# Converting float64 weights to float32 inside a Trainium2 kernel: a scaled absolute value in place of a raise and a mask

## The chip, the cores and the metric

The kernel runs on one core of a Trainium2 chip. A core has a matrix engine (PE), a vector engine (DVE), a scalar engine for activations and copies (ACT), a general one (POOL), and a queue of DMA issues on SyncE (SP). Each takes its instructions strictly in the order in which they stand in its program; semaphores hold an instruction until what it needs is there. The metric is the device time of one execution in microseconds.

## The reference, cut to what matters

Attention with packed queries p, then a mixer along the sequence (U, V) and a two-layer perceptron (w1, w2), for 8 batches, 8 heads, 576 rows, 64 columns a head.

```python
def _attn_ref(q, k, v, p):
    def sm_attn(qq, kk, vv):
        s = scale * np.matmul(qq, kk.transpose(0, 1, 3, 2))
        s = s - np.max(s, axis=-1, keepdims=True)
        a = np.exp(s)
        a = a / (np.sum(a, axis=-1, keepdims=True) + 1e-09)
        return np.matmul(a, vv)
    p_packed = sm_attn(p, k, v)
    out = sm_attn(q, p_packed, p_packed)

def _moe_ref(x, U, V, w_ch1, w_ch2):
    h = x.transpose(0, 2, 1) @ U @ V
    u = x + h.transpose(0, 2, 1)
    return u + np.maximum(u @ w_ch1, 0.0) @ w_ch2
```

q, k, v and p are float32. U, V, w1 (512 x 2048) and w2 (2048 x 512) are float64 and reach the kernel as pairs of 32-bit words; the kernel turns them into float32 itself, and this conversion is what the change is about.

## The kernel before, in words

**Stage 1 (to 98.3 us in the profile)** goes over 16 units, two for each batch. A unit loads its share of k (tile kx, three buffers, issue at L218) and of v (vt, three buffers, L425 and L427). It turns k by PE transposes (L229, L239) that ACT (L236, L240) and DVE (L234) copy out to kT. It forms scores with the packed queries (PE L249 into s_ps, one buffer), takes their maximum (DVE L460), the exponential (ACT L462), transposes it back (PE L255 and L257; ACT L471 and L474 copy it to eT), multiplies by v (PE L490), scales (ACT L492) and puts the heads in place (POOL L493, PE L500, ACT L501). Once a batch the packed queries are prepared: p is loaded (pn, one buffer, L415), doubled on POOL (L433, tile pd), transposed on PE (L435) and copied with the attention's scale by ACT (L436, L439) to pT, which both units of the batch use in L249.

Spread over the units stand 16 conversions of blocks of w1 (128 x 512 each), two small ones of U and V, and the conversion of w2's first block with its split into a high and a low part (ACT L165, and for this block POOL L166). With unit 13 the first fold is written: w1 times the packed result of batch 0 (PE L384), cut into a high part (ACT L390) and a low part (DVE L391). In stage 1 the order on each engine isn't that of the code: a scheduler places the instructions by their dependencies and its own costs, for the whole stage at once, so that a change in one operation's form can move others on every engine.

**Stage 2 (98.3 us to the end)** stands in the order in which it is written. It holds, for each batch, 16 pairs of a product with the folded w1 (PE L87 to L89 into h_ps, taken out by ACT L634 and L636 and DVE L637) and one with w2 (L87 to L89 into o). Between them stand the conversions of w2's other 15 blocks (up to about 180 us; the low half of their split is on DVE, L166), the steps of the next batch's attention, and the fold for what comes next. PE starts stage 2 with the first L87 into h_ps.

**A conversion** takes the high and the low word of each float64. It is called three ways: `convert_w1` (its Abs having been done ahead by `test_w1`, L150), `convert_w2` and `prepare_uv`. Before, it has one ACT instruction and four on DVE: Abs of the high word read as a float (L78 or L150), the raise to the least number that float32 shall hold (L79, `max`), the shift by 3 with a mask that keeps it clear of the sign (L80), the sign and top exponent bit from the high word (L81), and the top 3 bits of the low word (L82).

Of the kernel before, what the change touches and what calls it, by code (L numbers as in the profile page):

```python
# [9 lines left out]
F32 = mybir.dt.float32  # L10
F32R = mybir.dt.float32r
I32 = mybir.dt.int32
AF = mybir.ActivationFunctionType
ALU = mybir.AluOpType
# [6 lines left out]
def packed_attention_mixer_kernel(  # L21
# [27 lines left out]
    nc = tc.nc  # L49
# [13 lines left out]
    scale = 1.0 / float(D) ** 0.5  # L63
# [1 line left out]
    HALF = (slice(0, 5 * I), slice(5 * I, S))  # L65
    LAST = slice(4 * I, 5 * I)

    LEAST = 1.125 * 2.0 ** -15

    U, V, w1, w2 = (a.bitcast(I32) for a in (U, V, w1, w2))  # L70

    def float32_of(x, t, raw, out=None, tested=False):


        low, high = raw[:, :, 0], raw[:, :, 1]
        out = x if out is None else out.bitcast(I32)
        if not tested:
            nc.scalar.activation(t, high.bitcast(F32), AF.Abs)  # L78
        nc.vector.tensor_single_scalar(t, t, LEAST, op=ALU.max)  # L79
        nc.vector.tensor_scalar(x, t.bitcast(I32), 3, 0x3FFFFFF8, op0=ALU.logical_shift_left, op1=ALU.bitwise_and)  # L80
        nc.vector.scalar_tensor_tensor(x, high, -0x40000000, x, op0=ALU.bitwise_and, op1=ALU.bitwise_or)  # L81
        nc.vector.scalar_tensor_tensor(out, low, 29, x, op0=ALU.logical_shift_right, op1=ALU.bitwise_or)  # L82
        return out.bitcast(F32)

# [47 lines left out]
    def conv_tile(dtype):  # L132
        return pipe.tile([P, DM], dtype, name="os", bufs=4)
# [5 lines left out]
    bits = {}  # L139
# [6 lines left out]
    tests = {}  # L146

    def test_w1(n):
        tests[n] = conv_tile(F32)
        nc.scalar.activation(tests[n], bits["w1", n][:, :, 1].bitcast(F32), AF.Abs)  # L150

    def convert_w1(n):
        x, c = chunks[n]
        float32_of(conv_tile(I32), tests.pop(n), bits.pop(("w1", n)), w1t[x][:, QW * c:QW * c + QW], tested=True)
# [5 lines left out]
    def convert_w2(kt):  # L160
        return kt, float32_of(conv_tile(I32), conv_tile(F32), bits.pop(("w2", kt)))
# [26 lines left out]
    def prepare_uv(ub, vbits):  # L188
        ux = float32_of(conv_tile(I32)[:, :5 * R], conv_tile(F32)[:, :5 * R], ub.rearrange("p (x t) -> p x t", t=2))
        for (n, ks) in ((P, slice(0, 4)), (64, slice(4, 5))):  # L190
            nk = ks.stop - ks.start
            src = ux.rearrange("p (k r) -> p k r", k=5)[:n, ks].unsqueeze(2).to_broadcast([n, nk, 4, R])
            nc.vector.tensor_copy(ua4[:n, ks], src)
            nc.vector.tensor_tensor(ua4[:n, ks, 1], src[:, :, 0], ua4[:n, ks, 0].bitcast(F32), op=ALU.subtract)
        n = I // 2
        w = S // 4
        vq = float32_of(conv_tile(I32)[:, :w], conv_tile(F32)[:, :w], vbits.rearrange("p (x t) -> p x t", t=2))
        spread = x_tile()[:, :4 * P].rearrange("p (q a r) -> p q a r", q=4, a=4)
        nc.gpsimd.tensor_copy(spread, ident.rearrange("p (r q) -> p q r", q=4).unsqueeze(2).to_broadcast([P, 4, 4, R]))
        spread = spread.rearrange("p q a r -> p q (a r)")  # L200
        for hf in range(2):
            v_ps = bank()
            for y in range(2):
                nc.tensor.matmul(v_ps[:, w * y:w * y + w], lhsT=spread[:, 2 * hf + y], rhs=vq, start=True, stop=True)
            vx = v_ps[:, :2 * w].rearrange("p (i c) -> p i c", c=NT)
            blocks = vx[:, :, :8].rearrange("p i (a k r) -> p r k i a", a=2, k=2)
            ns = slice(n * hf, n * hf + n)
            pairs = [(vs[:, LAST][:, ns], vx[:, :, 8])]
            for r in range(2):
                dst = vs[:, HALF[r].start:HALF[r].start + 4 * I].rearrange("p (k i a) -> p k i a", k=2, a=2)[:, :, ns]  # L210
                pairs.append((dst, blocks[:, r]))
            for dst, src in pairs:
                nc.scalar.copy(dst, src)
                nc.vector.tensor_tensor(dst[96:], src[96:], dst[96:].bitcast(F32), op=ALU.subtract)
# [304 lines left out]
    a_turn(0)  # L519
    first = attention(0, res)  # L520
    test_w1(0)

    def some_w1(n):
        convert_w1(n)
        if n + 1 < 16:
            test_w1(n + 1)
        if n + 4 < 16:
            load_w1(n + 4)
# [182 lines left out]
    for b in range(B):  # L711
# [3 lines left out]
        for kt in range(NK):  # L715
# [17 lines left out]
            if kt % 4 == 2 and (b, kt) != (B - 1, NK - 2):  # L733
                n = b * NPC + kt // 4 + 1
# [58 lines left out]
```

## Time and profile before

| | us |
|---|---|
| time, median of 3 runs (829.01 to 829.96) | 829.05 |
| span of the profiled execution | 827.6 |
| stage 1, first load to first L87 | 98.3 |
| PE busy in the span | 799.1 |

One execution is profiled. Its span is the time from the first to the last recorded instruction; the time of a run includes a little around it. Timeline rows read: start in us, duration in us, engine, line, operation, output tile, input tiles, shape, count, and in brackets the engine's idle time before it with what ended it. In rows of groups, the count is followed by busy time in us and the mean duration in ns.

### The profile page before, as it was taken

To read this page: it belongs to the slowest core of one execution; us is meant where nothing else is said; L and a number is where in the kernel's file an instruction comes from. 1 tells how busy PE (TensorE), PEld (TensorE's weight loads), DVE (VectorE), ACT (ScalarE), POOL (GpSimd) and SP (SyncE) were. 2 spreads that over 40 slices of the span, in tenths; PEclk is the share of its full clock that TensorE was granted. 3 is DMA by queue.
4 is the path that set the end of the run, shared out by engine and by line. 5 is a ranking of instruction groups with operands and counts; after the bars stand their busy time and mean duration, and the time that the engine had idled before them with its cause. 6 is when DMAs were issued, how large, how long until landed. Compare 5 with 4: busy or idle time off the path is not lost.

```text
span 827.6 us, 15457 instructions
## 1 busy us (share of the span) xinstructions
PE 799.1 (97%) x6224; PEld 644.8 (78%) x6224; DVE 364.6 (44%) x815; ACT 319.8 (39%) x974; POOL 81.3 (10%) x115
## 2 busy tenths in 40 slices
PE   7788889999999999999999999999999999999997
PEld 5456567778888888888888888888888888887886
DVE  3789677783343333433334234333434234332232
ACT  5788764444223332333233232343234232332231
POOL 0222201100111001010101001010101011100000
PEclk8999999999999999999999999999999999999999
DMA  9999863216002220023002120122002200030001
GB/s 295 347 363 349 272 163 98 77 51 188 2 1 68 80 55 2 1 96 93 1 1 96 51 55 1 60 84 46 2 30 85 75 14 1 15 111 1 2 0 64
DMA packets 60310, 70.23 MB, mean 85 GB/s; under 512 B 22864, under 2 KB 41296, under 8 KB 60240
## 3 DMA queue, kind: packets, MB, share of 16 engines
q1 hardware_dynamic: 59920, 68.73, 26.6%
q8 instruction: 49, 0.80, 0.4%
q10 hardware_dynamic: 320, 0.52, 0.2%
q14 instruction: 21, 0.17, 0.1%
HBM read 53.64 MB, written 15.60 MB: 84 GB/s over the span
## 4 chain that ended last, share of the span: by engine, by line
PE 87%; DVE 5%; ACT 2%; DMA 1%; issue 1%; POOL 0%; ACTq 0%
PE o L87 16%; PE o L89 16%; PE o L88 16%; PE h_ps L87 9%; PE h_ps L89 8%; PE h_ps L88 8%; PE t_ps L384 4%; PE o L654 2%; PE t_ps L229 2%; PE t_ps L249 1%; DVE os L81 1%; PE t_ps L327 1%; PE t_ps L255 1%; DMA kx<-in_k_dram 1%; PE t_ps L344 1%
## 5 line engine op out<-in xcount | busy, mean ns | idle before, releaser
L87 PE MATMUL o<-w2h,hh 128*128 128x512 f32 x512 | 207.0, 404 | 0.0
L89 PE MATMUL o<-w2h,hl 128*128 128x512 f32 x512 | 202.9, 396 | 0.0
L88 PE MATMUL o<-w2l,hh 128*128 128x512 f32 x512 | 202.3, 395 | 0.0
L637 DVE SCALAR_TENSOR_TENSOR hl<-h_ps,hh 128x256 fp32r<-128x256 f32 x256 | 105.3, 423 | 203.3 <-ACT hj L636 189.3
L634 ACT ACTIVATE hh<-h_ps 128x256 fp32r<-128x256 f32 x256 | 98.8, 387 | 183.2 <-PE h_ps L89 182.5
L87 PE MATMUL h_ps<-ah,wth 128*128 128x320 f32 (+1 forms) x512 | 157.6, 308 | 0.8 <-DVE hl L637 0.8
L88 PE MATMUL h_ps<-al,wth 128*128 128x320 f32 (+1 forms) x512 | 151.5, 296 | 0.0
L89 PE MATMUL h_ps<-ah,wtl 128*128 128x320 f32 (+1 forms) x512 | 151.3, 296 | 0.0
L87 PEld LDWEIGHTS h_ps<-ah,wth 128*128 128x128 f32 x512 | 96.6, 189 | 26.2 <-issue 20.2
L89 PEld LDWEIGHTS o<-w2h,hl 128*128 128x128 f32 x512 | 96.6, 189 | 22.6
L87 PEld LDWEIGHTS o<-w2h,hh 128*128 128x128 f32 x512 | 97.3, 190 | 21.1 <-issue 4.6
L88 PEld LDWEIGHTS o<-w2l,hh 128*128 128x128 f32 x512 | 97.2, 190 | 16.8
L88 PEld LDWEIGHTS h_ps<-al,wth 128*128 128x128 f32 x512 | 96.8, 189 | 2.0
L89 PEld LDWEIGHTS h_ps<-ah,wtl 128*128 128x128 f32 x512 | 97.0, 189 | 0.0
L391 DVE TENSOR_TENSOR wtl<-t_ps,wth 128x256 fp32r<-128x256 f32 x128 | 48.5, 420 | 101.1 <-ACT wth L390 97.8
L390 ACT CAST wth<-t_ps 128x256 fp32r<-128x256 f32 x128 | 43.3, 374 | 109.3 <-PE t_ps L384 102.6
L347 POOL TENSOR_TENSOR al<-aT,ah 128x320 fp32r<-128x320 f32 (+1 forms) x32 | 25.7, 809 | 210.8 <-ACT ah L346 210.8
L290 POOL TENSOR_TENSOR e<-e,m 128x576 f32<-128x576 f32 x16 | 18.6, 1165 | 260.9 <-DVE m L289 259.1
L236 ACT COPY xT<-t_ps 128x256 f32<-128x256 f32 x64 | 21.3, 392 | 39.5 <-PE t_ps L229 38.8
L384 PE MATMUL t_ps<-w1t,ppT 64*32 64x512 f32 x512 | 34.9, 601 | 0.0
L346 ACT CAST ah<-aT 128x320 fp32r<-128x320 f32 (+1 forms) x32 | 13.8, 435 | 43.7 <-DVE aT L345 43.7
L636 ACT ACTIVATE hj<-h_ps 128x64 f32<-128x64 f32 x128 | 28.2, 220 | 0.0
(122 smaller groups left out, 838.3 us busy)
## 6 DMA issues: line engine op xcount, KB each, us to landing
bits<-in_moe_w_ch_dram SPq DMA_DIRECT2D x32, 512.0 KB, 6.2
kx<-in_k_dram SPq DMA_DIRECT2D x16, 576.0 KB, 7.2
x<-in_q_dram SPq DMA_DIRECT2D x16, 576.0 KB, 5.1
vt<-in_v_dram SPq DMA_DIRECT2D x32, 256.0 KB, 6.8
out_dram<-bits SPq DMA_DIRECT2D x32, 256.0 KB, 2.4
aD<-aT SPq DMA_DIRECT2D x16, 288.0 KB, 2.1
aP<-aD SPq DMA_DIRECT2D x32, 128.0 KB, 3.1
ppP<-ppD SPq DMA_DIRECT2D x32, 64.0 KB, 3.0
```

Of the source, the lines that this page charges most:

```text
L87: nc.tensor.matmul(ps, lhsT=lh, rhs=rh, start=start, stop=False)
L88: nc.tensor.matmul(ps, lhsT=lh, rhs=rl, start=False, stop=False)
L89: nc.tensor.matmul(ps, lhsT=ll, rhs=rh, start=False, stop=stop)
L236: nc.scalar.copy(dst, src[:, a])
L290: nc.gpsimd.tensor_tensor(e, e, m.unsqueeze(2).to_broadcast([P, S // 32, 32]), op=ALU.subtract)
L347: nc.gpsimd.tensor_tensor(al[:, g, ns], aT[:, ns], ah[:, g, ns].bitcast(F32), op=ALU.subtract)
L384: nc.tensor.matmul(f_ps[g][xs], lhsT=ppT[b][zs, g, xs], rhs=w1t[h // 2][zs, QW * c:QW * c + QW], start=True, stop=True)
L390: nc.scalar.copy(hi[:, g], f_ps[g][:, cs])
L391: nc.vector.tensor_tensor(lo[:, g], f_ps[g][:, cs], hi[:, g].bitcast(F32), op=ALU.subtract)
L634: nc.scalar.activation(hh[:, ms], src, AF.Relu)
L636: nc.scalar.activation(hj[:, jslot(self.b, kt), self.js], h_ps[:, LAST], AF.Relu)
L637: nc.vector.scalar_tensor_tensor(hl[:, ms], src, 0.0, hh[:, ms].bitcast(F32), op0=ALU.max, op1=ALU.subtract)
```

## The change

The Abs on ACT gets a scale of 2^-112, which its own instruction applies. With it the high word's exponent comes out in the place where float32 wants it, so the raise (L79) is gone, the shift (L80) has no mask any more and writes from the scaled value, and L81 takes the sign bit alone instead of the sign and the top exponent bit. Line numbers behind L79 stand as before; Abs inside `float32_of` is L79 after the change.

```diff
-    LEAST = 1.125 * 2.0 ** -15
+    REBIAS = 2.0 ** -112
+    SIGN = -0x80000000
...
         if not tested:
-            nc.scalar.activation(t, high.bitcast(F32), AF.Abs)
-        nc.vector.tensor_single_scalar(t, t, LEAST, op=ALU.max)
-        nc.vector.tensor_scalar(x, t.bitcast(I32), 3, 0x3FFFFFF8, op0=ALU.logical_shift_left, op1=ALU.bitwise_and)
-        nc.vector.scalar_tensor_tensor(x, high, -0x40000000, x, op0=ALU.bitwise_and, op1=ALU.bitwise_or)
+            nc.scalar.activation(t, high.bitcast(F32), AF.Abs, scale=REBIAS)
+        nc.vector.tensor_single_scalar(x, t.bitcast(I32), 3, op=ALU.logical_shift_left)
+        nc.vector.scalar_tensor_tensor(x, high, SIGN, x, op0=ALU.bitwise_and, op1=ALU.bitwise_or)
         nc.vector.scalar_tensor_tensor(out, low, 29, x, op0=ALU.logical_shift_right, op1=ALU.bitwise_or)
...
     def test_w1(n):
         tests[n] = conv_tile(F32)
-        nc.scalar.activation(tests[n], bits["w1", n][:, :, 1].bitcast(F32), AF.Abs)
+        nc.scalar.activation(tests[n], bits["w1", n][:, :, 1].bitcast(F32), AF.Abs, scale=REBIAS)
```

In stage 2 the rows on every engine are the same but for the L79 rows, which are gone. In stage 1 the scheduler places the work anew. The end of stage 1 shows it best, where the conversion of w2's first block (bits_1676 before, bits_1659 after) meets the packed queries of units 14 and 15 (pd and pT). Numbers in the names count tiles, and so differ between the two programs for the same thing: pd_1498 and pd_1484, pT_1497 and pT_1483, e1_1527 and e1_1513 (unit 13's exponential) go together.

On ACT, at the end of stage 1, this stood before:

```order
L78 ACTIVATE os_1687<-bits_1676 128x512
L236 COPY kT_1611<-k_ps_1612 128x2x128 x2
L462 ACTIVATE e1_1527,sm_1423<-s_ps_1483,sm_1423 128x576
L236 COPY kT_1611<-k_ps_1619 128x2x128
L436 ACTIVATE pT_1497<-t_ps_1496 128x128
L439 ACTIVATE pT_1497<-t_ps_1496 128x2x32 x2
L501 COPY ppTa_1560<-t_ps_1561 128x128
L477 ACTIVATE sm_1423<-sm_1423,eps_71 128x2
L492 ACTIVATE two_1557<-m_ps_1536,sm_1200 128x128
L240 COPY kT_1611<-k_ps_1626 64x4x64
L471 COPY eT_1586<-m_ps_1587 128x512
L165 CAST w2h0_102<-os_1686 128x512
```

And this stands there now:

```order
L236 COPY kT_1596<-k_ps_1597 128x2x128 x2
L462 ACTIVATE e1_1513,sm_1411<-s_ps_1469,sm_1411 128x576
L236 COPY kT_1596<-k_ps_1604 128x2x128
L477 ACTIVATE sm_1411<-sm_1411,eps_71 128x2
L492 ACTIVATE two_1542<-m_ps_1521,sm_1190 128x128
L240 COPY kT_1596<-k_ps_1611 64x4x64
L471 COPY eT_1571<-m_ps_1572 128x512
L79 ACTIVATE os_1670<-bits_1659 128x512
L474 COPY eT_1571<-m_ps_1578 64x128
L165 CAST w2h0_102<-os_1669 128x512
L436 ACTIVATE pT_1483<-t_ps_1482 128x128
L439 ACTIVATE pT_1483<-t_ps_1482 128x2x32 x2
```

The Abs of w2's first block has moved behind the copy of unit 13's transposed exponential (L471), and the scaled copies to pT (L436, L439) have moved behind the block's cast (L165). Behind them on ACT now follow unit 14's exponential and then the four casts of the fold, the two of one bank next to each other; before, the fold's casts stood on both sides of that exponential.

On POOL, at the same place, this stood before:

```order
L433 COPY pd_1498<-pn_1419 128x256
L347 TENSOR_TENSOR al_1261<-aT1_1132,ah_1260 128x320
L347 TENSOR_TENSOR al_1261<-aT0_926,ah_1260 128x256
L347 TENSOR_TENSOR al_1261<-aT1_1132,ah_1260 128x256
L493 COPY ppall_73<-two_1557 128x64
L166 TENSOR_TENSOR w2l0_103<-os_1686,w2h0_102 128x512
L493 COPY ppall_73<-two_1669 128x64
```

And this stands there now:

```order
L347 TENSOR_TENSOR al_1250<-aT1_1122,ah_1249 128x320
L347 TENSOR_TENSOR al_1250<-aT0_918,ah_1249 128x256
L347 TENSOR_TENSOR al_1250<-aT1_1122,ah_1249 128x256
L493 COPY ppall_73<-two_1542 128x64
L166 TENSOR_TENSOR w2l0_103<-os_1669,w2h0_102 128x512
L433 COPY pd_1484<-pn_1407 128x256
L493 COPY ppall_73<-two_1652 128x64
```

The doubling of p (L433) has moved from ahead of the mixer's subtractions (L347) to behind the low half of w2's first block (L166).

On PE, before, the transposes of pd (L435) stood well ahead of unit 14's scores (s_ps_1598):

```order
L435 MATMUL t_ps_1496<-ident_66,pd_1498 128x128 x2
L500 MATMUL t_ps_1561<-ident_66,two_1466 128x128
L490 MATMUL m_ps_1536<-vt_1173,eT_1375 32x64 x20
L239 MATMUL k_ps_1626<-ident_66,kx_1524 64x128 x2
L255 MATMUL m_ps_1587<-ident_66,e1_1527 128x128 x4
L249 MATMUL s_ps_1598<-kT_1505,pT_1497 32x320
```

Now they stand right ahead of them (s_ps_1583):

```order
L490 MATMUL m_ps_1521<-vt_1163,eT_1363 32x64 x20
L239 MATMUL k_ps_1611<-ident_66,kx_1510 64x128 x2
L255 MATMUL m_ps_1572<-ident_66,e1_1513 128x128 x4
L257 MATMUL m_ps_1578<-ident_66,e1_1513 64x128
L490 MATMUL m_ps_1631<-vt_1275,eT_1459 32x64 x20
L435 MATMUL t_ps_1482<-ident_66,pd_1484 128x128 x2
L500 MATMUL t_ps_1546<-ident_66,two_1452 128x128
L249 MATMUL s_ps_1583<-kT_1491,pT_1483 32x320
```

L435 has moved behind the products L490 of two units, and nothing but one transpose is left between it and the scores that need its result. On SP, the load of pn for these units stands behind the loads of v for units 12 and 13, and the load of w2's first block behind that of v for unit 12.

## Prediction

> **What bounds the kernel now.** First the page's totals, then a table of busy time by stretch.
>
> ```profile
> span 827.6 us, 15457 instructions
> PE 799.1 (97%) x6224; PEld 644.8 (78%) x6224; DVE 364.6 (44%) x815; ACT 319.8 (39%) x974; POOL 81.3 (10%) x115
> ```
>
> ```profile
> 26.00:42.00 16.00, 10.71 (x202) 7.25 (x200) 15.59 (x40) 12.05 (x41) 4.49 (x6) 1.00 1.08 336
> 58.00:75.00 17.00, 13.49 (x234) 9.02 (x233) 16.90 (x32) 13.13 (x43) 4.57 (x8) 0.90 1.06 355
> 200.00:821.00 621.00, 619.96 (x4286) 509.62 (x4285) 219.64 (x509) 196.02 (x603) 50.64 (x60) 1.00 0.13 40
> ```
>
> Behind the stretch and its length stand the busy times of PE, weight load, DVE, ACT and POOL, then granted clock, DMA share and GB/s. From 200 to 821 us PE works 619.96 of 621.00 us, so nothing that DVE saves there can shorten it; the conversions are over by then anyhow. In stage 1, two stretches are DVE's: 15.59 of 16.00 us and 16.90 of 17.00 us. The DMA share is above 1 in both, so transfers stand close behind. How close, the last load of k tells.
>
> ```profile
> 76.19 0.41 SPq L218 DMA_DIRECT2D kx<-in_k_dram  x1
> DMA to landing us min/median/max: 5.7/7.1/7.3
> 88.43 1.09 PE L229 MATMUL k_ps<-ident,kx 128*128 128x128 f32 x8
> ```
>
> Issued at 76.19, it lands by 83.5 (76.19 + 7.3), and PE turns it at 88.43. Stage 1 thus runs **4.9 us** behind its data at that point. That is the most that faster conversions can win before stage 2, as long as bytes set the landing.
>
> **The change part by part.**
>
> ```profile
> L79 DVE TENSOR_SCALAR os<-os 128x512 f32<-128x512 f32 x32 | 14.2, 445 | 3.2 <-ACT os L150 2.4 <-ACT os L78 0.2
> L80 DVE TENSOR_SCALAR os<-os 128x512 int32<-128x512 int32 x32 | 13.5, 423 | 0.8
> L436 ACT ACTIVATE pT<-t_ps 128x128 f32<-128x128 f32 x8 | 2.3, 282 | 5.8 <-PE t_ps L435 5.8
> L501 ACT COPY ppTa<-t_ps 128x128 f32<-128x128 f32 x14 | 3.9, 278 | 3.5 <-PE t_ps L500 3.5
> L165 ACT CAST w2h<-os 128x512 fp32r<-128x512 f32 x16 | 9.9, 621 | 10.0 <-DVE os L82 10.0
> L78 ACT ACTIVATE os<-bits 128x512 f32<-128x512 f32 x16 | 10.8, 678 | 0.0
> ```
>
> *Prices of single operations.* L79 goes: 32 instructions, 14.2 us of DVE, besides two small ones. L80 keeps one of its two operations. L79 has one operation and takes 445 ns, L80 has two and takes 423, so the second costs nothing I can see: I take 0, between -22 and +22 ns (0.7 us of DVE over 32). Abs gets a constant scale. L436 multiplies by a constant and takes 282 ns where L501, a plain copy of the same size, takes 278: 4 ns an Abs, taken as 0. The widest distance that the rows offer is that from the cast L165 (621) to today's Abs of the same size (678), 57 ns.
>
> The Trainium skill, "ScalarE: Activation LUTs", section "What ACT_TABLE_LOAD costs", says that an activation with a constant scale and bias has the smaller fixed cost and that each operand read through a pointer adds about 93 ns. If the new scale came as a pointer, 34 Abs would by that page take some 3.2 us more of ACT (an estimate); the two rows above speak for a constant.
>
> *Stage 1, relief.* Of L79 alone, the two stretches that DVE fills hold this (busy us and count behind the length):
>
> ```profile
> 26.00:42.00 16.00, 1.80 (x5) 1.00 1.08 336
> 58.00:75.00 17.00, 1.97 (x5) 0.90 1.06 355
> ```
>
> Together 3.8 us. What is late next when that goes is ACT (13.13 of 17.00) and the data, so not all of it comes through: I take **-3.0 us**, with 0 and -4.9 as ends.
>
> *Stage 1, the tail.* The scheduler places stage 1 anew, and one piece of its end is worse: the conversion of w2's first block (its Abs on ACT, six instructions on DVE, L165 on ACT, the low half L166 on POOL) now stands ahead of the scaled copy of p for units 14 and 15 (L433 on POOL, L435 on PE, L436 and L439 on ACT). Before, L433 was long done. Now it is behind L166 on POOL, and L436 behind L165 on ACT; behind L435 on PE stand the scores of unit 14 (L249), the fold, and all of stage 2.
>
> ```profile
> 90.98 0.31 ACT L436 ACTIVATE pT<-t_ps 128x128 f32<-128x128 f32 x1
> 91.14 0.36 ACT L439 ACTIVATE pT<-t_ps 128x64 f32<-128x64 f32 x2
> 92.20 0.64 ACT L471 COPY eT<-m_ps 128x512 f32<-128x512 f32 x1
> 93.18 0.62 ACT L165 CAST w2h<-os 128x512 fp32r<-128x512 f32 x1 [0.34 <-DVE os L82]
> ...
> 90.25 0.76 DVE L80 TENSOR_SCALAR os<-os 128x512 int32<-128x512 int32 x2
> 90.92 1.28 DVE L81 SCALAR_TENSOR_TENSOR os<-bits,os 128x512 int32<-128x512 int32 x2
> 92.46 0.68 DVE L82 SCALAR_TENSOR_TENSOR os<-bits,os 128x512 int32<-128x512 int32 x1
> ...
> 85.79 0.40 POOL L433 COPY pd<-pn 128x256 f32<-128x256 f32 x1
> 93.88 1.26 POOL L166 TENSOR_TENSOR w2l<-os,w2h 128x512 fp32r<-128x512 f32 x1 [1.47 <-ACT w2h L165]
> ...
> 89.36 0.38 PE L435 MATMUL t_ps<-ident,pd 128*128 128x128 f32 x2
> 91.49 0.76 PE L249 MATMUL s_ps<-kT,pT 64*32 64x320 f32 x16
> 98.33 0.41 PE L87 MATMUL h_ps<-ah,wth 128*128 128x320 f32 x1
> ```
>
> On the old clock, relief left out: Abs now follows the L471 copy, which ended at 92.84. With the old Abs (0.68) no longer ahead of it, and L436 and L439 gone from there, the copy ends near 92.0, no sooner, because it also waits for PE's transposes. Then Abs 0.68, the two interleaved conversions on DVE up to L82 2.63 (90.25 to 92.20, and 0.68), L165 0.62, L166 1.26, L433 0.40, L435 0.38, L436 and L439 0.52 (90.98 to 91.50): 92.0 + 6.5 = **98.5** for the scores of unit 14, which ran at 91.49. From there to the first multiplication of stage 2 (98.33) it was 6.84 us; now these follow one another:
>
> ```profile
> 93.72 0.75 DVE L460 TENSOR_REDUCE sm<-s_ps 128x1 f32<-128x576 f32 x1
> 94.39 0.41 DVE L391 TENSOR_TENSOR wtl<-t_ps,wth 128x256 fp32r<-128x256 f32 x1
> ...
> 93.70 0.37 ACT L390 CAST wth<-t_ps 128x256 fp32r<-128x256 f32 x1
> 94.51 0.74 ACT L462 ACTIVATE e<-s_ps,sm 128x576 f32<-128x576 f32 x1 [0.44 <-DVE sm L460]
> 95.92 0.31 ACT L477 ACTIVATE sm<-sm,eps 128x1 f32<-128x1 f32 x1
> ```
>
> Scores 0.76, maximum 0.75 (no longer behind conversions on DVE), exp 0.74, L477 0.31, then the fold's four casts and four subtractions, now behind the exp on ACT and taking turns on a bank: 3 x 0.37 + 4 x 0.41 = 2.75; one more transpose 0.38. That is 5.7, so stage 2 starts at 104.2: **+5.9 us** before the relief. If the scores' inputs came as early as before, this term would be 0.
>
> The load of pn is moved too, behind v of unit 13:
>
> ```profile
> 85.48 0.61 SPq L427 DMA_DIRECT2D vt<-in_v_dram  x1
> ```
>
> Issued near 86.1 and landed by 93.4 (7.3 later), it is there before POOL comes to L433 at 97.2; without that cover it would cost nothing until it was 3.8 us later. The load of w2's first block moves behind one load of v; it is still early for an Abs at 92.0.
>
> *The clock.* PE now idles some 5 us in one piece ahead of L435. What an idle piece does, stage 2 shows:
>
> ```profile
> 123.52 0.77 PE L249 MATMUL t_ps<-xT,ppT 64*32 64x320 f32 x16 [2.22 <-ACT xT L240]
> 124.00:130.00 6.00, 5.62 (x29) 4.02 (x20) 4.81 (x11) 1.49 (x4) 0.00 (x0) 0.72 0.35 100
> ```
>
> After 2.22 us of waiting the granted clock averaged 0.72 from 124 to 130 us, though PE was at work for 5.62 of the 6.00; that is 0.28 x 6 = 1.7 us of full clock lost. For the new idle piece I add **+0.7**, between 0 and 1.7, since much of what follows it waits on ACT and DVE anyhow.
>
> The Trainium skill, "TensorE: Matmul & The Clock Gate", Part 1, has the rate halved only after one whole idle window of about 3.4 us, and the windows run free of the program; by that rule a gap of 5 us would hold a whole one in about half the cases, 0.8 us on the mean (an estimate). The trace does not agree on the condition, since the clock fell behind a gap of 2.22 us; by the trace any such gap may cost its 1.7, and the sum would be 1.0 higher.
>
> *ACT's backlog.* The casts of the fold push ACT's last L471 and exp into the time when stage 2's first products must be evacuated: 0.64 + 0.74, with some PE work beside it; I take half, **+0.7** (0 to 1.4).
>
> *Stage 2.* Order is unchanged but for L79. These PE stalls end on a chain with a conversion in it:
>
> ```profile
> 110.40 0.30 PE L257 MATMUL t_ps<-ident,e 128*64 128x128 f32 x1 [0.29 <-ACT xT L236]
> 126.76 0.48 PE L500 MATMUL t_ps<-ident,two 128*128 128x128 f32 x1 [0.38 <-DVE e L283]
> 167.27 0.42 PE L87 MATMUL h_ps<-ah,wth 128*128 128x320 f32 x1 [0.49 <-DVE hl L637]
> 122.02 0.62 ACT L165 CAST w2h<-os 128x512 fp32r<-128x512 f32 x1 [2.43 <-DVE os L82]
> ```
>
> At 123.52 PE waits for L240, which stands behind L165, which waits for L82; one L79 (0.45) out of that chain saves 0.45, and the rest of the 2.22 stays. With 0.29, 0.38 and at most 0.45 of 0.49: **-1.6** (0 to -2.0). If that shorter stall no longer lowers the clock, its 1.7 go too: half of that, **-0.8** (0 to -1.7). Elsewhere in stage 2, PE's own work hides L79; where that cover is gone, it is the 0.45 a block counted here.
>
> *Sum:* 5.9 - 3.0 + 0.7 + 0.7 - 1.6 - 0.8 = **+1.9 us**. The profiled span is 827.6; the median of the three runs, 829.05, has 1.45 us around it, which the change does not touch. So 829.5 for the span and **831.0** for the time.
>
> **Rivals.**
>
> *The relief runs through to the data.* DVE's full stretches are the only hold on stage 1, and it catches up the whole 4.9 us: 831.0 - 1.9 = 829.1, no change. For it: of the 32 large L79, 17 stand in stage 1 (w1's 16 and w2's first), 17 x 0.445 = 7.6 us, twice the 3.8 counted. Against it: ACT is at 13 of 17 us.
>
> *Faster.* The landing of the last kx at 83.5 is set by the buffer it waits for and not by bytes. Then quicker units issue the loads earlier too, stage 1 has no floor at 4.9, and a relief of 7 us, most of those 7.6, gives 831.0 - 4.0 = 827.0. It decides from a landing before about 81.4, the 2.1 that 7 needs beyond 4.9. Against it: a DMA share of 1.06 to 1.08 throughout.
>
> *No relief.* ACT and data hold stage 1 as they do DVE, and only the tail remains: 831.0 + 3.0 = 834.0. Against it: DVE's 16.90 of 17.00.
>
> *The scaled Abs is dearer than the old one.* By the widest distance above it is 0.057 x 34 = 2 us, half of it on the path: 832.0. Against it: 282 beside 278.
>
> **How the numbers follow.** Chances: forecast 0.45, relief to the data 0.25, faster 0.12, no relief 0.12, dearer Abs 0.06. About 0.2%, 1.7 us, is what a measurement of this kernel can tell from no change: below 827.4 is faster, above 830.7 slower. The forecast's own range is 829.6 to 832.5; a quarter of it (0.11) falls within 0.2%. The second case is 0.06 on the faster side and the rest within. So faster 0.18, same 0.30, slower 0.52. The range leaves out about 0.1 below 827.0, where only the third case goes, and 0.1 above 834.0.
>
> **What the changed profile would show.** The tail: POOL's L433 right behind L166, and PE's L435 with an idle of some 5 us ahead of it, released by POOL. Were L433 early, that term falls and the time is near 825. The relief: the last turn of kx less than 2 us behind its landing. The clock: granted clock well under 1 near 98 us or not, and 1.00 near 126. Stage 2: the wait at L249 about 1.8 in place of 2.22. A group mean of Abs above 690 ns, or of L80 away from 423, would upset the prices. PE from 200 to 821 us must stay as it is; if it doesn't, the forecast is wrong from the ground.

## The result, and the profile after

| | before | after |
|---|---|---|
| time, median of 5 runs (us) | 829.08 (829.01 to 829.96) | 833.45 (831.53 to 834.14) |
| span of the profiled execution (us) | 827.6 | 829.7 |
| first L87 of stage 2 in it (us) | 98.33 | 103.53 |
| from there to the last instruction's start (us) | 729.22 | 726.14 |

The changed kernel is slower: the ratio of its time to that of the kernel before is 1.0047, 95% interval 1.0035 to 1.0059. Measured once more beside other kernels (run e11) it is 1.0038, 1.0027 to 1.0049. The profiled execution, 831.53, is the fastest of its five. It loses 5.2 us before stage 2 begins and gains 3.1 us within it.

The table of busy time by stretch (stretch and length, then PE, weight load, DVE, ACT, POOL, granted clock, DMA share, GB/s); first one row of before, then the rows of after:

```profile
88.40:98.30 9.90, 8.41 (x197) 5.35 (x193) 7.83 (x17) 8.87 (x30) 3.27 (x6) 1.00 0.94 292
```

```profile
26.00:42.00 16.00, 12.63 (x212) 8.64 (x210) 13.97 (x35) 12.63 (x46) 4.27 (x6) 1.00 1.08 337
58.00:75.00 17.00, 14.05 (x224) 9.37 (x217) 15.22 (x29) 13.09 (x41) 3.87 (x6) 0.90 1.07 357
88.40:98.30 9.90, 4.66 (x77) 2.64 (x80) 4.16 (x9) 3.64 (x13) 2.07 (x4) 0.72 0.95 295
200.00:821.00 621.00, 619.97 (x4289) 510.09 (x4289) 219.73 (x509) 196.70 (x605) 50.56 (x60) 1.00 0.13 41
```

The two stretches that DVE filled have 1.6 and 1.7 us of it free now, and from 200 us on PE's busy time has changed by 0.01 us. The loss stands in the third row: from 88.4 to 98.3 us PE works 4.66 us where it worked 8.41, DVE, ACT and POOL are each idle for more than half of the time, and the granted clock is 0.72.

What they wait for is read from the timeline of after, engine by engine (start, duration, engine, line, operation, output and inputs, idle time before it and what ended it):

```profile
89.65 0.70 ACT L79 ACTIVATE os<-bits 128x512 f32<-128x512 f32 x1
92.98 0.62 ACT L165 CAST w2h<-os 128x512 fp32r<-128x512 f32 x1 [2.48 <-DVE os L82]
96.05 0.28 ACT L436 ACTIVATE pT<-t_ps 128x128 f32<-128x128 f32 x1 [2.46 <-PE t_ps L435]
...
90.38 0.76 DVE L80 TENSOR_SCALAR os<-os 128x512 int32<-128x512 int32 x2 [1.23 <-ACT os L79]
92.26 0.69 DVE L82 SCALAR_TENSOR_TENSOR os<-bits,os 128x512 int32<-128x512 int32 x1
...
93.68 1.26 POOL L166 TENSOR_TENSOR w2l<-os,w2h 128x512 fp32r<-128x512 f32 x1 [4.32 <-ACT w2h L165]
94.88 0.40 POOL L433 COPY pd<-pn 128x256 f32<-128x256 f32 x1
...
95.33 0.69 PE L435 MATMUL t_ps<-ident,pd 128*128 128x128 f32 x2 [4.62 <-POOL pd L433]
96.38 1.32 PE L249 MATMUL s_ps<-kT,pT 64*32 64x320 f32 x16 [0.15 <-ACT pT L436]
103.53 0.39 PE L87 MATMUL h_ps<-ah,wth 128*128 128x320 f32 x1
```

One engine after the other works while the rest waits: Abs at 89.65, DVE until 92.95 (for this block), the cast on ACT until 93.60, the low half on POOL until 94.9, then the doubling of p, which needs nothing of all that and only stands behind it: its own data, issued at 84.12, had landed 6.6 us later, at 90.7. PE sits idle for 4.62 us, and the scores of unit 14 run at 96.38 instead of 91.49.

### The profile page after: what moved, and what is told of

The parts are those of the page before. It is cut to its first block, busy times and chain, and to the rows that moved or that the text cites. A ratio compares the mean times of both kernels' runs of the same rounds, so it can differ in the third digit from the quotient of the medians.

```text
span 829.7 us, 15436 instructions
## 1 busy us (share of the span) xinstructions
PE 798.7 (96%) x6224; PEld 643.7 (78%) x6224; DVE 351.2 (42%) x781; ACT 318.7 (38%) x974; POOL 80.1 (10%) x115
## 4 chain that ended last, share of the span: by engine, by line
PE 89%; DVE 4%; DMA 3%; ACT 2%; issue 1%; POOL 0%; SPq 0%; ACTq 0%; POOLq 0%
PE o L87 16%; PE o L89 16%; PE o L88 16%; PE h_ps L87 9%; PE h_ps L89 8%; PE h_ps L88 8%; PE t_ps L384 4%; DMA bits<-in_moe_w_ch_dram 2%; PE o L654 2%; PE t_ps L229 2%; DMA vt<-in_v_dram 1%; PE t_ps L327 1%; PE t_ps L249 1%; PE t_ps L255 1%; DVE os L81 1%
## 5 line engine op out<-in xcount | busy, mean ns | idle before, releaser
L87 PE MATMUL o<-w2h,hh 128*128 128x512 f32 x512 | 206.6, 404 | 0.0
L87 PE MATMUL h_ps<-ah,wth 128*128 128x320 f32 (+1 forms) x512 | 157.7, 308 | 0.4 <-DVE hl L637 0.3
L87 PEld LDWEIGHTS h_ps<-ah,wth 128*128 128x128 f32 x512 | 96.7, 189 | 25.6 <-issue 21.0
L87 PEld LDWEIGHTS o<-w2h,hh 128*128 128x128 f32 x512 | 97.0, 189 | 21.0 <-issue 4.6
L390 ACT CAST wth<-t_ps 128x256 fp32r<-128x256 f32 x128 | 43.3, 374 | 110.0 <-PE t_ps L384 102.3
L347 POOL TENSOR_TENSOR al<-aT,ah 128x320 fp32r<-128x320 f32 (+1 forms) x32 | 25.7, 806 | 211.5 <-ACT ah L346 211.5
```

What stands on the lines that cost most here:

```text
L87: nc.tensor.matmul(ps, lhsT=lh, rhs=rh, start=start, stop=False)
L347: nc.gpsimd.tensor_tensor(al[:, g, ns], aT[:, ns], ah[:, g, ns].bitcast(F32), op=ALU.subtract)
L390: nc.scalar.copy(hi[:, g], f_ps[g][:, cs])
```

## The experiments

Each is compared with the kernel before on the same chip. Ratios are to it, with their 95% intervals; the changed kernel's was 1.0047 at first and 1.0038 in e11. Line numbers in some of these kernels are a few higher than in the kernel before.

### e1 and e2: one stage at a time

The conversion gets a switch, and one stage uses the old form. For e1, set against the changed kernel:

```diff
-        nc.scalar.activation(tests[n], bits["w1", n][:, :, 1].bitcast(F32), AF.Abs, scale=REBIAS)
+        nc.scalar.activation(tests[n], bits["w1", n][:, :, 1].bitcast(F32), AF.Abs)
...
-        return kt, float32_of(conv_tile(I32), conv_tile(F32), bits.pop(("w2", kt)))
+        return kt, float32_of(conv_tile(I32), conv_tile(F32), bits.pop(("w2", kt)), old=kt == 0)
```

The conversions of w1, U and V have `old=True` too. For e2 it is `old=kt > 0`, and w1, U and V are new. The order of stage 1 is that of before in e1 and that of the changed kernel in e2, row for row.

> The new conversion only for w2's blocks 1 to 15 (stage 2); w1, U, V and w2's first block are converted as before, and stage 1 stands in the order of before. Theory (the loss is the tail of stage 1, the gain of stage 2 stands by itself): stage 2 starts at 98.3 us as before, its stalls shrink by 1.4 us, and by 1.7 more if the clock no longer falls near 126: 826.0 to 827.7 us. Rival A (the new arithmetic is itself dearer, 15 of 32 blocks of it): over 830. Rival B (stage 2 gained only because it started later): 829.1, no change.

> The new conversion only in stage 1 (w1, U, V, w2's first block), in the changed kernel's order; w2's blocks 1 to 15 are converted as before. Theory: first multiplication of stage 2 at 103.5 us, stage 2 as before: 829.1 + 5.2 = 834.3, or 832.6 if the clock doesn't fall near 126. Rival (the loss arises in stage 2): 829 or less.

e1: 827.17 us median, ratio 0.9974 (0.9964 to 0.9983). e2: 834.05 us, 1.0062 (1.0047 to 1.0077). The product of the two ratios is 1.0036, close to the whole change (1.0038 and 1.0047). First the timeline of e1, then that of e2, PE's rows:

```profile
97.67 0.41 PE L93 MATMUL h_ps<-ah,wth 128*128 128x320 f32 x1
121.92 0.77 PE L255 MATMUL t_ps<-xT,ppT 64*32 64x320 f32 x16 [1.77 <-ACT xT L246]
```

```profile
95.49 0.69 PE L441 MATMUL t_ps<-ident,pd 128*128 128x128 f32 x2 [4.62 <-POOL pd L439]
103.69 0.39 PE L93 MATMUL h_ps<-ah,wth 128*128 128x320 f32 x1
128.86 0.77 PE L255 MATMUL t_ps<-xT,ppT 64*32 64x320 f32 x16 [2.21 <-ACT xT L246]
```

With the new conversion in stage 2 (e1), its long stall is 1.77 us and not 2.22, though stage 2 starts no later than before; with the old one there (e2) it is 2.21, though stage 2 starts at 103.69. So stage 2's gain belongs to the arithmetic, and the loss to stage 1, where e2 repeats the wait of 4.62 us. Of the rivals, dearer arithmetic is out, and so are a gain that comes only from a later start and a loss that arises in stage 2. One caution for all that follows: e1 starts stage 2 at 97.67 and the kernel before at 98.33, in the same order; so the start times of two single executions can differ by 0.7 us without any cause in the program.

### e3 and e8: the wait undone, and half of it

e3 only swaps two places, on POOL the doubling of p ahead of the low half and on ACT pT's copies ahead of the cast (`ready` holds the last doubling and the last copy, and `issue_after` puts what follows behind an instruction on that one's engine); e8 moves the low half to DVE and leaves ACT's order.

```diff
 e3
-            split_w2(*convert_w2(0))
+            x = convert_w2(0)
+            with tc.issue_after(ready[-1][0]), tc.issue_after(ready[-1][1]):
+                split_w2(*x)
 e8
-        (nc.gpsimd if kt == 0 else nc.vector).tensor_tensor(lo, x, hi.bitcast(F32), op=ALU.subtract)
+        nc.vector.tensor_tensor(lo, x, hi.bitcast(F32), op=ALU.subtract)
```

> The changed kernel with two places swapped back: on POOL the doubling of p for units 14 and 15 ahead of the low half of w2's first block, on ACT its scaled copies ahead of the block's cast. All else stands as in the changed kernel. Theory: the doubling starts when p has landed (90.7 us), the scores of unit 14 run near 92.5 instead of 96.4, their maximum at 93.6 behind the conversion instead of 97.8, stage 2 starts 4 to 5 us earlier, and the clock doesn't fall there: 826.5 to 829.0 us. Rival A (the wait is not what costs, another part of the new order is): 831.5 to 834. Rival B (relief comes to nothing without the wait's slack): 829 to 831.

> The changed kernel with the low half of w2's first block on DVE instead of POOL; ACT's and PE's order stay as in the changed kernel. The doubling of p no longer waits behind it on POOL (only for its data, landed at 90.7), but pT's copies still stand behind the block's cast on ACT, which ends at 93.6. Theory (two waits in a row, POOL's 1.3 + 0.4 + 0.7 and ACT's): scores of unit 14 near 94.2 instead of 96.4, stage 2 about 2 us earlier. Rival (ACT's order alone sets it): scores stay at 96.4. Rival (POOL's alone): scores near 92.5.

e3: 828.68 us, 0.9998 (0.9987 to 1.0010). e8, a single run: 830.82 us. The timelines of e3 and then of e8:

```profile
91.73 0.43 POOL L433 COPY pd<-pn 128x256 f32<-128x256 f32 x1 [2.23 <-DMA pn<-in_p_dram]
...
93.01 0.77 PE L249 MATMUL s_ps<-kT,pT 64*32 64x320 f32 x16 [0.26 <-ACT pT L436]
99.61 0.39 PE L87 MATMUL h_ps<-ah,wth 128*128 128x320 f32 x1
...
93.89 0.76 DVE L463 TENSOR_REDUCE sm<-s_ps 128x1 f32<-128x576 f32 x1
```

```profile
92.14 0.44 PE L435 MATMUL t_ps<-ident,pd 128*128 128x128 f32 x2 [0.74 <-POOL pd L433]
94.72 1.31 PE L249 MATMUL s_ps<-kT,pT 64*32 64x320 f32 x16 [2.02 <-ACT pT L436]
101.86 0.39 PE L87 MATMUL h_ps<-ah,wth 128*128 128x320 f32 x1
```

In e3 nothing differs from the changed kernel's order in stage 1 but the two swapped places; stage 2 starts 3.9 us earlier, and the time is that of before. These two places account for the whole net loss. They don't account for the rest: relief and stage 2's gain would make e3 faster than before, and it isn't, since stage 2 still starts at 99.61 and not before 98.33. Three things stand right behind the wait: p's own load, which lands when POOL has waited 2.23 us for it, the conversion on DVE, behind which unit 14's maximum runs only at 93.89, and the granted clock, which fell to a half here too, from 94.0 to 97.4 us, against the expectation. e8 shows the wait as two in a row. POOL's part gone, L435 runs at 92.14 and the scores at 94.72, in the middle between 93.01 and 96.38; 2.02 us of idle PE are left, for pT's copies behind the cast on ACT. Rivals that gave the cost to one engine alone fall. Stage 2 starts 1.7 us earlier than in the changed kernel, a little less than the 2 expected.

### e5 and e6: the load of p early

```diff
+            if i == 12:
+                a_load(i + 2)
-            a_load_v(i + 1)
+            with tc.issue_after(pload[-1]) if i == 12 else ExitStack():
+                a_load_v(i + 1)
...
+            with tc.issue_after(pload[-1]):
+                load_w2(0)
+                load_w2(1)
+                steps = attention(1, res)
+                steps.pop(0)()
```

`pload` holds the loads of p. e5 is the changed kernel with this edit, e6 the kernel before with it.

> The changed kernel with one edit on the load queue: the load of p for units 14 and 15 is issued ahead of the load of v for unit 13, and of w2's and q's loads behind it, instead of after them. Nothing is pinned on the engines; with this the scheduler itself puts the doubling of p ahead of the low half of w2's first block, and pT's copies ahead of the block's cast. Theory (the late place of that small load is what made the scheduler turn the tail around; relief and stage 2's gain are whole without it): no idle gap ahead of the doubled p's transposes, scores of unit 14 near 91.7 us, stage 2 from 97.0 to 98.0, time 825.0 to 827.5. Rival A (the tail stays late for another reason, such as the data): as e3, 828.7. Rival B (the gain belongs to the edit and not to the change): the same edit in the kernel before gains as much.

> The kernel before with the same edit on the load queue as the changed kernel has in the run beside it. Theory: the doubling of p was never late there, so little changes: 828.0 to 829.5 us, start of stage 2 near 98. Rival (the edit alone is what helps): 826.5 or less, and the run beside it is no better.

e5: 829.27 us, 1.0000 (0.9991 to 1.0010). e6: 829.80 us, 1.0008 (1.0000 to 1.0017). The timeline of e5, one row of DVE, two of ACT and one of PE:

```profile
95.42 0.75 DVE L462 TENSOR_REDUCE sm<-s_ps 128x1 f32<-128x576 f32 x1
...
95.53 0.62 ACT L165 CAST w2h<-os 128x512 fp32r<-128x512 f32 x1 [0.23 <-DVE os L82]
96.20 0.74 ACT L464 ACTIVATE e<-s_ps,sm 128x576 f32<-128x576 f32 x1
...
97.09 1.11 PE L255 MATMUL m_ps<-ident,e 128*128 128x128 f32 x4 [4.29 <-ACT e L464]
```

The doubled p came early, as the theory had it, the scores were through at 92.8, and still the forecast of 825.0 to 827.5 missed. The scheduler now had unit 14's maximum behind the block's conversion on DVE and its exponential behind the block's cast on ACT; the idle piece of 4.62 us came back as one of 4.29 us, one step further down. So it isn't the doubling of p that is special. Whatever of the units' chain stands behind a link of this conversion waits for all links up to it. The traced execution of e5, 831.07, is the slowest of its eleven, and the granted clock in it is a half from 95.8 to 105.9 us; so its start of stage 2, 101.58, is later than is typical for this kernel, by how much isn't known. e6 shows that the edit alone wins nothing; its 829.80 is just above the 829.5 expected, and in its trace stage 2 starts at 100.14, not near 98.

### e9, e10 and e12: the conversion elsewhere

```diff
 e9, e10
-            split_w2(*convert_w2(0))
+            with tc.issue_after(top), tc.issue_after(ex):
+                split_w2(*convert_w2(0))
 e12
-        nc.scalar.activation(tests[n], bits["w1", n][:, :, 1].bitcast(F32), AF.Abs, scale=REBIAS)
+        nc.scalar.activation(tests[n], bits["w1", n][:, :, 1].bitcast(F32), AF.Abs, **(dict(scale=REBIAS) if n >= 8 else {}))
```

`top` and `ex` are unit 14's maximum and exponential. In e12 the first 8 conversions of w1 take the old form in their DVE part, too. e9 and e10 also have the early load of p, e10 as in e5, e9 behind w2's first block.

> The changed kernel with two edits: the load of p for units 14 and 15 is issued ahead of v for unit 13 and of q (behind w2's first block, whose load stays early), and the conversion of w2's first block is put behind unit 14's maximum on DVE and behind its exponential on ACT. In e5 the wait had only moved: the maximum of unit 14 stood behind the conversion on DVE (95.42) and its exponential behind the block's cast on ACT (96.20), 4.3 us of idle PE. Theory (whatever of the units' chain stands behind this conversion waits for all of it): scores of unit 14 near 91.5, maximum at 92.2, exponential at 93, no idle piece of PE above 1.5 us, stage 2 from 96.5 to 98, and then a small wait of its first evacuation for the block's cast; 825.5 to 827.5 us. Rival (the tail is bound by something else, for instance the fold's casts and the last loads of v): stage 2 not before 99.5, 828.5 or more.

> As e9, but the load of p goes ahead of the load of w2's first block and of q as well, as in e5. That block's data then lands some 5 us later, near 90; it isn't needed before 93. Theory: as e9 within 1 us, 825.5 to 828. Rival (w2's first block comes too late for the first multiplication with w2, near 100): 1 to 2 us more than e9.

> The new conversion everywhere but in the first 8 of w1's 16 blocks, which are converted as before. With this mix the scheduler loads w2's first block ahead of the last k and converts it two units earlier, right behind unit 11's exponential; at the end of stage 1 the doubled p, pT's copies, unit 14's maximum and exponential have no conversion ahead of them. Theory (the loss is where the scheduler puts this one conversion; the new arithmetic gains wherever its order is harmless): last k lands 1 to 1.5 us later, stage 2 starts from 96.0 to 98.0, no idle piece of PE above 2 us from 85 us on, stage 2 as in the changed kernel: 825.0 to 827.5 us, as good as e1 or better. Rival (moved to unit 12 the conversion costs there what it cost at unit 14): stage 2 not before 99, 828.5 or more.

e9: 829.35 us, 1.0002 (0.9992 to 1.0011). e10: 828.24 us, 0.9988 (0.9979 to 0.9997). e12: 831.40 us, 1.0022 (1.0011 to 1.0034). One PE row of e9 and one of e10, then two rows of e12:

```profile
99.07 0.81 PE L503 MATMUL t_ps<-ident,two 128*128 128x128 f32 x2 [1.57 <-DVE wtl L391]
```

```profile
100.53 0.41 PE L87 MATMUL h_ps<-ah,wth 128*128 128x320 f32 x1 [1.50 <-DVE hl L645]
```

```profile
88.06 0.62 ACT L171 CAST w2h<-os 128x512 fp32r<-128x512 f32 x1 [2.06 <-DVE os L88]
88.91 0.77 PE L255 MATMUL s_ps<-kT,pT 64*32 64x320 f32 x16 [0.92 <-ACT pT L442]
```

All three missed their forecasts of 825 to 828, and the figures of the rivals of e9 (stage 2 not before 99.5) and e12 (not before 99) came in, with 99.53 and 102.92. Put last, the conversion meets the fold on DVE (1.57 us in e9) or stage 2's first evacuations (1.50 us in e10, which starts stage 2 at 97.17 and gives much of it back). e10 also has PE idle for 1.99 us at 94.23, ahead of the conversion, for the fold's own casts and subtractions in turn; so the fold is a limit of its own right behind the conversion. Put two units earlier, the conversion holds pT's copies of unit 12 (0.92 us of idle PE). But e12 was late before that: its granted clock was a half for 13.7 us between 36 and 78 us, against 3.4 us in the kernel before, and its last k is turned only from 91.33 on, against 88.43 before. What share of e12's lag each of these has was not settled. e10 has the lowest time with the new form everywhere (its interval and e3's overlap), and the fastest of all is e1.

### e4 and e7: the clock in the gap

Useless products fill PE's wait for the doubled p, 34 in e4 (the expectations say 33) and 16 in e7. Here is e4's edit.

```diff
+        if u == 12:
+            for _ in range(34):
+                nc.tensor.matmul(p_ps[:, 2 * P:3 * P], lhsT=ident, rhs=ident, start=True, stop=True)
         two = ua[u]["two"] = sT.tile([P, 2, D], F32, name="two")
```

> The changed kernel with 33 matrix multiplications of no use (into an unused part of a bank) put into PE's idle gap ahead of the doubled p's transposes. The wait stays, only PE isn't idle in it; a few rows of the fold behind it change places. Theory (part of the loss is the clock that falls behind the gap, and its chance position is what spreads the times from 831.5 to 834.1): granted clock stays 1.00 from 90 to 100 us, stage 2 starts about 1 us earlier, 830.5 to 832.5 us with a spread below 1 us. Rival (the clock falls for reasons outside the gap, or costs nothing there): 833.4 with the same spread.

> As e4, with 16 multiplications instead of 33, since 33 (two passes each) took 7.6 us and kept PE past the end of the wait; 16 take about 3.7 us of the gap of 4.6. Theory (the fallen clock costs 1.3 us between unit 14's scores and stage 2, 7.15 us at half clock against 5.84 in e4): granted clock 1.00 from 90 to 100, scores at 96.2, stage 2 near 102.1, time 1.3 below the changed kernel's: about 832.1. Rival (the stretch behind the scores is bound by ACT and DVE, not by the clock): stage 2 at 103.5, 833.4.

e4: 833.58 us (833.00 to 833.68, four runs), 1.0053 (1.0038 to 1.0068), which misses its forecast of 830.5 to 832.5. e7: 832.64 us (829.86 to 834.63), 1.0042 (1.0029 to 1.0055). PE's rows of after, then those of e7:

```profile
96.38 1.32 PE L249 MATMUL s_ps<-kT,pT 64*32 64x320 f32 x16 [0.15 <-ACT pT L436]
99.48 0.66 PE L255 MATMUL m_ps<-ident,e 128*128 128x128 f32 x4
102.62 0.90 PE L490 MATMUL m_ps<-vt,eT 128*32 128x64 f32 x40 [0.83 <-ACT eT L471]
```

```profile
91.08 3.84 PE L493 MATMUL m_ps<-ident 128*128 128x128 f32 x32
96.59 0.77 PE L249 MATMUL s_ps<-kT,pT 64*32 64x320 f32 x16 [0.26 <-ACT pT L436]
99.14 0.66 PE L255 MATMUL m_ps<-ident,e 128*128 128x128 f32 x4 [0.93 <-ACT e L462]
102.27 1.45 PE L490 MATMUL m_ps<-vt,eT 128*32 128x64 f32 x40 [0.83 <-ACT eT L471]
```

In after the granted clock is a half from 92.7 to 99.5 us; in e7 it is full until 102.3, in the same order but for the useless products. From the scores to unit 14's transposes it is 3.10 us at half clock and 2.55 at full, and to the last L490 6.24 and 5.68: the fallen clock costs about **0.55 us** here, not the 1.3 that e4 seemed to show (e4's order behind the scores differs by a few rows, and its products kept PE busy for 7.6 us, past the wait). Ahead of the scores it costs another 0.24: from L435 to them it is 1.05 us (95.33 to 96.38) in after and 0.81 (95.78 to 96.59) in e7. In e7 the clock fell later instead, from 102.3 to 105.7, over the last product of stage 1 and stage 2's first ones, and stage 2 started at 103.78, not at the 102.1 expected. In this execution filling the gap moved the fall rather than removing it. The spread is not cured: of e7's ten runs the two with a mean granted clock of 0.997 and above took 829.86 and 830.14 us, and the two at 0.988 took 834.03 and 834.63.

### e11: the changed kernel once more

> The changed kernel once more, beside the others on the same chip. Theory: L435's idle near 4.6 us, stage 2 from 103.4 to 103.8, 831.5 to 834.1 us, and granted clock at a half near 92 to 99 us. Rival (the first measurement was a chance of the chip): 829 to 831.

832.40 us (830.65 to 833.81), 1.0038. L435 again waits for 4.62 us. Stage 2 starts at 103.24, 0.2 us ahead of the range expected, and the clock is a half from 94.4 to 101.2 us. The loss is the kernel's.

## Why the prediction was right, and where its sizes were off

The forecast was 831.0 within 827.0 to 834.0, slower, by a wait at the end of stage 1. Each step, in its own order:

**Prices of single operations: right for Abs and for the sum, not for L80 alone.** The groups of after:

```profile
L80 DVE TENSOR_SCALAR os<-os 128x512 int32<-128x512 int32 x32 | 15.2, 476 | 7.5 <-ACT os L150 6.1 <-ACT os L79 1.2
L81 DVE SCALAR_TENSOR_TENSOR os<-bits,os 128x512 int32<-128x512 int32 x32 | 22.2, 696 | 0.8
L79 ACT ACTIVATE os<-bits 128x512 f32<-128x512 f32 x16 | 10.8, 678 | 0.0
```

Abs takes 678 ns with the scale and took 678 without it. L79, L80 and L81 took 445, 423 and 748; L80 and L81 now take 476 and 696. That L80 has left 423 upsets the price of L80 alone; the block is 444 ns cheaper, which is the removed L79.

**Relief, -3.0: too large.** The last turn of kx in after:

```profile
75.80 0.39 SPq L218 DMA_DIRECT2D kx<-in_k_dram  x1
86.19 1.09 PE L229 MATMUL k_ps<-ident,kx 128*128 128x128 f32 x8
```

That is 2.24 us earlier than before. Over executions it is less: 88.43 and 87.78 with the old stage 1 (before, e1), 85.50 to 86.88 with the changed kernel's (after, e2, e3, e4, e7, e8, e11; mean 86.25), so **1.9 us**. The sign that the prediction named failed as well: the turn is not less than 2 us behind the landing but 4.0 (86.19 behind 82.2), because the landing itself came 1.3 us earlier in this execution. Between the same executions it lies from 82.2 to 83.8, on the mean at 83.1 with the old stage 1 and 82.9 with the changed one; so on the mean the turn is still 3.4 us behind it. What holds stage 1 back between the removed 3.8 us and the 1.9 that came through was not isolated; the prediction named ACT.

**The tail, +5.9: right in mechanism, a little small.** From Abs to the scores the sum was 6.5 us and it is 6.73 (89.65 to 96.38), of which 0.24 is the clock; Abs itself, forecast at 92.0 less the relief, came at 89.65. From the scores to stage 2 the sum was 5.7, and it is 7.15, of which 0.55 is the clock. Of the missing 0.9, some 0.6 is the step that the prediction put as "one more transpose", 0.38 us, and that took 1.00 (the last subtraction ends at 102.53, stage 2 starts at 103.53): behind the fold's casts on ACT also stands L471, and PE's last product L490 waits for it. The remaining 0.3 is short gaps between the steps. These two rows of after are the last cast and the copy behind it:

```profile
101.70 0.37 ACT L390 CAST wth<-t_ps 128x256 fp32r<-128x256 f32 x1 [0.55 <-DVE wtl L391]
101.97 0.59 ACT L471 COPY eT<-m_ps 128x512 f32<-128x512 f32 x1
```

**The clock, +0.7: right,** 0.8 in this execution (0.55 and 0.24). **ACT's backlog, +0.7: not there:** the first stall of stage 2 is 0.34 us in after and was 0.33. The late L471 that this term was made of shows ahead of stage 2 instead, in the 0.6 of the tail.

**Stage 2, -1.6: about right; the -0.8 by luck.** The stalls at 110.40, 167.27 and 171.17 are gone (0.29, 0.49 and 0.20), the long one is 1.77 instead of 2.22, and the next, whose 0.38 the prediction counted as saved, is 0.43: 1.4 us. The clock stayed full behind the shorter stall, which is 1.7 more and makes up the 3.1. That was luck: of the ten profiles with a long stall of 1.76 or 1.77 us the clock fell behind it in five (e3, e7, e8, e11, e12) and not in the other five (after, e1, e5, e9, e10). Nor did the longer stall always lower it: behind 2.22 and 2.21 us (before, e2) it fell, behind 2.23 (e6) it didn't. So it isn't shown that the change saves any of these 1.7 us on the mean. e1, whose stage 1 is the old one, shows what is left over many runs: 1.8 us by the medians.

*Sum:* -2.2 (relief) + 5.9 + 0.9 (tail) + 0.8 (clock) make 5.4 at the start of stage 2, measured 5.2; and -3.1 behind it. The forecast had 4.3 and -2.4 for these two. The profiled execution is thus 2.1 us longer in span where 1.9 was forecast, but the closeness is luck: the two misses, 0.9 more and 0.7 less, nearly cancel. The time adds a third, small one: the prediction took 1.45 us from the span to the time, a median of three runs less the span of one, while in every run with both figures the time is 1.7 to 1.9 us above its own span. By the ratios the kernel is 3.2 to 3.9 us slower than before, more than the 1.9 forecast, and the clock is the likely rest: the profiled execution has the highest mean granted clock of its five, 0.990 against 0.985 to 0.989, and the gain of 1.7 near 126 us is not there in e11. That is argued from means and not shown by a trace of a slower run of the first measurement.

**"Were L433 early, the time is near 825": wrong.** e3, e5, e9 and e10 have it early and take 828.2 to 829.4. The step priced the wait as if nothing stood behind it, but p's load, DVE's conversion, the block's cast and the fold do, one after the other. Of the rivals, the relief did not run through to the data (the turn stays 3.4 us behind); the last kx's issue hardly moved (75.80 for 76.19) and its landing at 82.2 isn't before the 81.4 that "faster" asked for; some relief came; and Abs was not dearer.

## What to carry to other kernels

Where a scheduler sets the order, taking an instruction out of a helper is also a new order everywhere: read the new rows at the stage's end, and look for an engine's row that needs nothing of the row ahead of it. A chain that crosses engines (here Abs, DVE, cast, low half) delays whatever is placed behind one of its links by the sum of all links up to that one, and moving one victim ahead shows the next. If the old order was good and one stage's gain is safe, change that stage alone: e1, with the new form only in the stage whose order is written by hand, is the fastest kernel here, 0.9974; of the others only e10, 0.9988, has an interval that stays below 1.

## What the runs showed of the hardware that had not been expected

The granted clock can fall to a half behind PE gaps much shorter than the time for which it then stayed low, and whether it fell was not set by the length of the gap just ahead. Behind 1.76 us it fell in e3 and not in e9, behind 1.77 us it fell in e11 and not in e1, and behind 2.23 us in e6 it didn't. Behind the 4.62 us of the changed kernel it fell in after and e11, but 2.0 and 4.0 us after the gap had begun. It stayed at a half for 3.4, 6.8 or, in e5, 10.2 us.

How often it falls seems to make much of the spread between runs of one kernel, 4.8 us in e7, where time and mean granted clock go closely together. This is seen in the means only, and it isn't all: a run of e11 with a mean of 0.993, the highest of its ten, took 833.25 us, close to the slowest.

And single prices moved without the sum: L81, untouched but for its constant, went from 748 to 696 ns when the instruction ahead of the pair was removed, and L80, which lost its mask, from 423 to 476.
